# Taps' maxima in PSUM beside two tiles' results, the subtraction on VectorE, the first taps ahead of the weights' loads, and a new order

## The chip, the core and the metric

The kernel runs on one core of a Trainium2 chip. A core has five engines with instruction queues of their own that run side by side: PE (TensorE, matrix products into PSUM), DVE (VectorE), ACT (ScalarE), POOL (GpSimd) and SP (SyncE, which here issues most DMAs). Each engine takes its instructions strictly in the order in which the program lists them, and waits on semaphores for the others. PSUM has banks of 512 fp32 numbers in each of 128 partitions.

The metric is the device time of one execution in microseconds (us). Before the change it is 1347.68 us, the median of three runs (1347.58 to 1349.73).

## The reference

Two stages over 8 x 4160 = 33280 tokens of width 192: a local attention with given weights, and a feed-forward product with a gated softmax and a norm.

```python
w = exp(weight_gen - max(weight_gen))                  # over the 7 taps, for 8 heads
w = w / (sum(w) + 1e-09)
x = einsum('bshk,bskhg->bshg', w, windows(x, 7))       # each token: 7 taps over itself and its 6 predecessors

h = x @ w_in                                           # 192 -> 1024
e = exp(h - max(h))
solu = h * e / (sum(e) + 1e-09)
ln = (solu - mean(solu)) / sqrt(var(solu) + 1e-06) * g_ln
out = ln @ w_out                                       # 1024 -> 192
```

## The kernel before

A partition holds 260 consecutive tokens, and a *tile* t is the t-th token of all 128 partitions, so there are 260 tiles. Inputs come in *chunks*, of 4, 8 and 8 tiles at first and then of 16 tiles each. For each chunk `softmax_taps` (L102) makes the attention weights in seven steps, t0 to t6, in place in the tile `wt`: t0 the maximum over 7 taps (DVE, L112, into the tile `wm`), t1 the subtraction (POOL, L114), t2 the exponential (ACT, L118), t3 the sum (DVE, L120), t4 a small constant added (ACT, L122, into `wy`), t5 the reciprocal (DVE, L124), t6 the multiplication (POOL, L126).

The attention itself runs on POOL in groups of 4 tiles (2 at the start): a multiplication of seven windows of x with the taps into `pr` (L174), an addition (L180) and another into `half` (L182). DVE adds the last two parts (L433).

For each tile there follow:

- PE transposes two tiles' x at once (L450); ACT rounds a high part (L458) and DVE takes the rest (L479);
- the first product (L491, L494), 12 matmuls in three high-low pairings, into one of three buffers `h` of two PSUM banks;
- the negated maximum (DVE, L505), the exponential with its sum (ACT, L509), the product h times e (DVE, L515), the sum of squares (ACT, L521);
- a split into two fp16 halves, high (ACT, L528) and low (DVE, L532), in the tile `hl`, which a DMA transposes into `hlT` (L540);
- the second product (L580), 24 matmuls into `po`, a PSUM bank, and the scaled output (ACT, L591, into `ot`), which a DMA stores for four tiles at a time (L594).

Row norms for the chunk (`norm_x`, L136) and per-tile scales (`scales`, L544, for groups of `stat_group` tiles) are small instructions between these. The weights arrive as float64 and are turned into fp32 by DVE and ACT in pieces during the first 60 us (`float_of_double`, L232, and the steps behind it).

`po` has one buffer. The sums and norms that are needed for the weights use the same bank early on. The order of nearly all instructions is made by `issue_order` (L660): a list scheduler over estimated costs, in which a table `URGENCY` shifts the priority of each kind of step. Its result is one list of steps. Each engine's queue is that list restricted to the engine, and where two steps of different engines touch the same PSUM tile, the later one in the list waits for the earlier one. Outside that list, ahead of it, stand the first loads and, behind the weights' loads, the taps of chunk 0 (L227).

Of the kernel before, what the change touches and what calls it, by code (L numbers as in the profile page):

```python
# [9 lines left out]
F32 = mybir.dt.float32  # L10
# [16 lines left out]
def tile_kernel(ctx: ExitStack, tc: tile.TileContext, x, weight_gen, w_in, w_out, g_ln, out):  # L27
# [26 lines left out]
    ps_o = ctx.enter_context(tc.tile_pool(name="ps_o", bufs=1, space=PSUM))  # L54

    nc.scalar.preload_act_table_set("natural_log_exp_and_others")

# [44 lines left out]
    def softmax_taps(c, step):  # L102
        n = (starts[c + 1] - starts[c]) * H
        w3 = ws[c][:, : n * K].rearrange("p (n k) -> p n k", k=K)
        if step == 0:
            m = small.tile([P, TC * H], F32, name="wm", bufs=2)[:, :n]
            y = small.tile([P, TC * H], F32, name="wy", bufs=2)[:, :n]
            taps[c] = m, y
        m, y = taps[c]
        wide = [P, n, K]  # L110
        if step == 0:
            nc.vector.tensor_reduce(m, w3, axis=AX.X, op=ALU.max)  # L112
        elif step == 1:
            nc.gpsimd.tensor_tensor(  # L114
                out=w3, in0=w3, in1=m.unsqueeze(2).broadcast_to(wide), op=ALU.subtract
            )
        elif step == 2:
            nc.scalar.activation(w3, w3, AF.Exp)  # L118
        elif step == 3:
            nc.vector.tensor_reduce(m, w3, axis=AX.X, op=ALU.add)  # L120
        elif step == 4:
            nc.scalar.activation(y, m, AF.Copy, bias=1e-9)  # L122
        elif step == 5:
            nc.vector.reciprocal(y, y)  # L124
        elif step == 6:
            nc.gpsimd.tensor_tensor(  # L126
                out=w3, in0=w3, in1=y.unsqueeze(2).broadcast_to(wide), op=ALU.mult
            )
# [60 lines left out]
    w_out = w_out.bitcast(I32)  # L189
    load_x(0)  # L190
    raw_a = att.tile([P, 2 * FF], I32, name="raw_a", bufs=1)

# [32 lines left out]
    nc.vector.tensor_scalar_mul(minus, ident, -1.0)  # L225

    for step in range(TAP_STEPS):  # L227
        softmax_taps(0, step)

# [52 lines left out]
    def norm_of_first(step):  # L282
# [5 lines left out]
        elif step == 3:  # L288
            nc.scalar.activation(sq[:, 4:7], sq[:, 4:7], AF.Square)
        elif step == 4:  # L290
            first["total"] = ps_o.tile([P, 512], F32, name="po")
            nc.tensor.matmul(first["total"][:, :3], ones, sq[:, 4:7], start=True, stop=True)
        elif step == 5:
            nc.vector.tensor_reduce(
                first["total"][:, 8:9], first["total"][:, :3], axis=AX.X, op=ALU.add
            )
        elif step == 6:
            nc.scalar.activation(column, first["total"][:, 8:9], AF.Ln, scale=1.05 * FF)
            nc.scalar.activation(column, column, AF.Exp, scale=0.5)
# [27 lines left out]
    def scale_and_sum(f, step):  # L327
# [10 lines left out]
        elif step == 1:  # L338
            if f == 0:
                second["sums"] = ps_o.tile([P, 512], F32, name="po")  # L340
            for j in range(j0, j1):
# [10 lines left out]
    def prepare_second(step, half=None):  # L352
# [8 lines left out]
        elif step == 5:  # L361
            second["total"] = second["sums"][:, 256:]
            nc.tensor.matmul(second["total"][:, :NP], ones, sq[:, :NP], start=True, stop=True)
# [42 lines left out]
    def stat_group(t):  # L406

        n = 2 if t < 2 * TG else TG
        return n if t % n == n - 1 else 0


    def group(t):

        if t < TG:
            return 2 if t % 2 == 0 else 0
        return TG if t % TG == 0 else 0
# [156 lines left out]
    def second_product(t):  # L573
        hlT = hlT_of.pop(t)

        free = t >= RUN - TG and t % 2 == 1
        po = ps_h.tile([P, FF], F32, name="h") if free else ps_o.tile([P, 512], F32, name="po")
        terms = [(half, j, w) for j in range(NJ) for half, w in ((0, 0), (0, 1), (1, 0))]
# [66 lines left out]
URGENCY = dict(  # L645
    a00=3.1, a01=2.3, a02=-28.9, a03=-6.5, a04=-3.6, a10=80, a11=-25.4, a12=-13, a13=-10, a14=10.4,
    attA=85.1, attB=2.4, b0=120.9, b1=-144.6, b2=138.3, b3=-1.5, b4=54.3, c00=-28.1, c01=85.1,
    c02=6.8, c10=-25.3, c11=31.3, c12=-72.7, c20=99.4, c21=-5.6, c22=10.2, c30=-149.7, c31=-14.5,
    c32=-100.3, dup=52.6, exp=-129.5, f0=8.2, f1=-120.4, f2=-71.5, f3=-118.4, f4=-66.1, f5=-45.6,
    fin=18.4, hi=-11, lo=33, lw=18.7, lx0=10.2, lx1=-115.4, lx2=-109.1, lx3=-20.7, max=-30,  # L650
    mm1=25.5, mm2=0.4, n0=-7.5, n1=11.8, n2=-1.8, n3=-113.6, n4=-8.6, n5=-69, n6=-123.6, od=-6.9,
    out=-81.2, p30=22.9, p31=0.5, p4=9.7, p5=12.6, p6=11.6, p70=-10.2, p71=-8.7, p80=20.3, p81=5.9,
    q00=7.1, q01=-5.1, q02=118.9, q10=-15.7, q11=20.7, q12=16.8, q20=100.6, q21=-95.2, q22=20.4,
    q30=143.8, q31=81.5, q32=98.3, solu=-7.6, sq=5, t0=5.1, t1=-3.7, t2=77.9, t3=44.1, t4=-26.5,
    t5=110.1, t6=267.2, tr=-13, v00=170.9, v01=5.1, v02=44, v03=0.2, v1=54.2, v2=58.8, v3=-12.2,
    v4=1, v5=21.2, xT=-66.9, xhi=-46.7, xld=30,
)


def issue_order(run, starts, group, stat_group, loads):  # L660
# [7 lines left out]
    SAME, CROSS = (25, 127, 143, 0, 102), 130  # L668
    free = [3000, 5900, 5000, 12000, 9050]
    steps, number = [], {}  # L670
# [10 lines left out]
    for n, part in enumerate(parts):  # L681
        w_in, size = n < 3, 512 if n < 3 else 384
        at = (9000, 10500, 12000)[n] if w_in else 15000
        before = () if w_in else (f"{parts[n - 3]}4", "n" + {"a0": "0", "a1": "1", "b": "2"}[parts[n - 3]]) if n < 6 else ("q00",)
# [9 lines left out]
        else:  # L694
            f = n - 3
            once(f"q{f}0", ACT, 700, part + "2")
            once(f"q{f}1", PE, 660, f"q{f}0", *([f"q{f - 1}1"] if f else ["n6"]))
# [35 lines left out]

    add("v00", 0, ACT, 1800, ready=9000)
    add_norms(0, 0)
    for c in range(1, len(starts) - 1):
# [8 lines left out]
        for part in range(4 if whole else 1):  # L745
# [5 lines left out]
            else:  # L751
                add(f"v0{part}", t, ACT, size, ready=15000)
        add_norms(c, t)
        n = (starts[c + 1] - t) * 8
        on = (DVE, POOL, ACT, DVE, ACT, DVE, POOL)
        wide = 60 + 7.3 * n
        costs = (wide, 13.5 * n, 100 + 6 * n, wide, 100 + n, 60 + 6.3 * n, 13.5 * n)
        for k in range(7):
# [4 lines left out]
            else:  # L763
                add("t0", t, on[k], costs[k], ready=12000)

# [3 lines left out]
    for i, t in enumerate(groups):  # L769
# [4 lines left out]
        if c > 1:  # L774
            after.append((f"lx{loads - 1}", starts[c]))
        add("attA", t, POOL, 14990 if full else 7500, *after, ready=15000 if c == 1 else 9000)
        add("attB", t, POOL, 3510 if full else 1800, ("attA", t), ("fin", groups[i - 2] if i > 1 else -1))
# [21 lines left out]
    for t in range(run):  # L799
# [13 lines left out]
        add("tr", t, SP, 1792, ("lo", t), ("mm2", t - 6))  # L813
        after = [("p80", 0), ("p81", 0)] if t == 0 else []
        if t >= run - 4:
            after += [("mm1", run - 1), ("out", t - 2)]
        else:
            after.append(("out", t - 1))
        add("mm2", t, PE, 2170, ("tr", t), *after)
        add("out", t, ACT, 304, ("mm2", t), ("f5", stats_of[t]), ("od", t // 4 * 4 - 5))  # L820
        if n := stat_group(t):
# [103 lines left out]
```

## Time and profile before

| | |
|---|---|
| median of three runs | 1347.68 us |
| the profiled execution | 1347.67 us |
| its span, first to last instruction | 1345.8 us |
| mean granted TensorE clock | 0.994 |
| HBM read and written | 46.15 MB and 25.56 MB |

A row of the profile's costliest groups names the line, the engine, the operation, what it writes and reads, how often it ran, the busy us of all, the mean ns of one, and the idle time ahead of it with what ended it. Busy shares of stretches of the span (stage rows) tell where the kernel is limited by what. All durations come from the one profiled execution.

### The profile page before, as it was taken

What the parts mean: (1) busy time and instruction counts of PE and PEld (TensorE: products, weight loads), DVE (VectorE), ACT (ScalarE), POOL (GpSimd) and SP (SyncE); (2) the same over time, 40 slices, a digit from 0 to 9 for tenths busy, and PEclk for the clock granted to TensorE, in tenths of its full rate; (3) what the DMA queues carried; (4) which work ended last, traced back from release to release, by engine and by line L of the source; (5) the groups of instructions that cost most, each with busy time, mean ns of one, the idle gap of its engine ahead of it and who ended that gap; (6) DMA issues with size and microseconds to landing.
All of it is one profiled execution on the core that took longest, in us unless ns stands there. A gap on an engine that the chain in (4) does not pass through costs nothing.

```text
span 1345.8 us, 25810 instructions
## 1 busy us (share of the span) xinstructions
PE 1246.8 (93%) x9900; PEld 970.8 (72%) x9900; DVE 1210.2 (90%) x1588; ACT 1162.8 (86%) x2318; POOL 1247.7 (93%) x241
## 2 busy tenths in 40 slices
PE   0588899999999999999999999999999999999997
PEld 0365677777777777777777777777777777777776
DVE  5988899999999999999999999999999999889994
ACT  3778889889898988989898998989898898988886
POOL 5989899999999999999999999999999999999930
PEclk9899999999999999999999999999999999999999
DMA  5277668797886889688797968878787877976776
GB/s 180 74 159 169 139 134 201 123 207 137 155 179 134 196 137 208 125 179 163 129 202 140 191 140 180 162 128 203 140 193 137 183 150 138 183 134 123 133 134 130
DMA packets 565307, 210.31 MB, mean 156 GB/s; under 512 B 544456, under 2 KB 545864, under 8 KB 565184
## 3 DMA queue, kind: packets, MB, share of 16 engines
q1 hardware_dynamic: 563208, 206.55, 75.7%
q10 hardware_dynamic: 1976, 2.12, 0.6%
q8 instruction: 78, 1.28, 0.4%
q14 instruction: 45, 0.37, 0.1%
HBM read 46.15 MB, written 25.56 MB: 53 GB/s over the span
## 4 chain that ended last, share of the span: by engine, by line
ACT 43%; DVE 35%; issue 11%; PE 7%; DMA 2%; POOL 1%; SPq 0%; ACTq 0%; POOLq 0%
ACT hl L528 12%; ACT e L521 12%; DVE h L515 11%; DVE hl L532 11%; ACT e L509 9%; DVE stats L505 5%; DVE a L433 4%; ACT junk L145 3%; PE po L580 3%; PE h L494 2%; ACT x_hi L458 2%; ACT ot L591 2%; DMA hlT<-hl 2%; PE h L491 1%; DVE x_lo L479 1%
## 5 line engine op out<-in xcount | busy, mean ns | idle before, releaser
L174 POOL TENSOR_TENSOR pr<-xt,wt 128x5376 f32<-128x5376 f32 (+1 forms) x66 | 631.6, 9569 | 2.7
L580 PE MATMUL po<-w_hl,hlT 128*128 128x192 f16 x6192 | 555.1, 246 | 17.3 <-ACT ot L591 12.6
L580 PEld LDWEIGHTS <-hlT 128*128 128x128 f16 x6240 | 505.9, 98 | 83.2 <-issue 75.5
L515 DVE SCALAR_TENSOR_TENSOR h<-h,row,e 128x1024 f32<-128x1024 f32 x260 | 333.8, 1285 | 19.1 <-ACT e L509 16.9
L528 ACT ACTIVATE hl<-h 128x1024 f16<-128x1024 f32 x260 | 266.0, 1029 | 98.4 <-DVE h L515 55.4
L532 DVE SCALAR_TENSOR_TENSOR hl<-h,hl 128x1024 f16<-128x1024 f32 x260 | 316.5, 1218 | 36.8 <-ACT e L521 34.4
L180 POOL TENSOR_TENSOR pr<-pr 128x2304 f32<-128x2304 f32 (+1 forms) x66 | 333.0, 5045 | 5.2
L505 DVE TENSOR_REDUCE stats<-h 128x1 f32<-128x1024 f32 x260 | 316.3, 1217 | 3.9 <-PE h L494 3.3
L509 ACT ACTIVATE e<-h,stats 128x1024 f32<-128x1024 f32 x260 | 293.3, 1128 | 16.1 <-DVE stats L505 15.5
L521 ACT ACTIVATE e<-h,stats 128x1024 f32<-128x1024 f32 x260 | 293.0, 1127 | 1.1 <-DVE hl L532 1.0
L494 PE MATMUL h<-wa_hi,x_hi 128*128 128x512 f32 x520 | 234.0, 450 | 0.0
L182 POOL TENSOR_TENSOR half<-pr 128x1536 f32<-128x1536 f32 (+1 forms) x66 | 225.8, 3421 | 5.2
L494 PE MATMUL h<-wa_lo,x_hi 128*128 128x512 f32 x520 | 206.4, 397 | 0.0
L494 PE MATMUL h<-wa_hi,x_lo 128*128 128x512 f32 x520 | 205.9, 396 | 0.0
L494 PEld LDWEIGHTS h<-wa_hi,x_hi 128*128 128x128 f32 x520 | 98.1, 189 | 107.1 <-issue 95.5
L491 PE MATMUL h<-wb_hi,x_hi 64*128 64x512 f32 x520 | 131.0, 499 | 17.1 <-DVE hl L532 11.2
L433 DVE TENSOR_REDUCE a<-half 128x768 f32<-128x1536 f32 (+1 forms) x66 | 117.2, 1776 | 0.0
L591 ACT ACTIVATE ot<-po,stats 128x192 f32<-128x192 f32 x258 | 112.4, 436 | 3.6 <-PE po L580 3.6
L494 PEld LDWEIGHTS h<-wa_hi,x_lo 128*128 128x128 f32 x520 | 98.4, 189 | 23.2
L494 PEld LDWEIGHTS h<-wa_lo,x_hi 128*128 128x128 f32 x520 | 99.0, 190 | 12.0
L491 PE MATMUL h<-wb_hi,x_lo 64*128 64x512 f32 x520 | 104.2, 395 | 0.0
L450 PE MATMUL pa<-ident,a 128*128 128x128 f32 x520 | 81.2, 278 | 23.9 <-DVE x_lo L479 13.2
(89 smaller groups left out, 1072.0 us busy)
## 6 DMA issues: line engine op xcount, KB each, us to landing
out_dram<-ot SPq DMA_DIRECT2D x65, 384.0 KB, 3.3
xt<-in_x_dram SPq DMA_DIRECT2D x30, 576.0 KB, 4.8
xt<-in_x_dram SPq DMA_DIRECT2D x30, 480.0 KB, 4.4
wt<-in_weight_gen_dram SPq DMA_DIRECT2D x15, 448.0 KB, 4.8
hlT<-hl SPq DMA_TRANSPOSE x260, 4.7
xt<-in_x_dram SPq DMA_DIRECT2D x3, 384.0 KB, 4.6
raw_a<-in_moe_w_in_dram ACTq DMA_DIRECT2D x2, 512.0 KB, 7.4
raw<-in_moe_w_out_dram ACTq DMA_DIRECT2D x1, 768.0 KB, 12.2
```

The lines of the kernel that those rows point to most:

```text
L174: nc.gpsimd.tensor_tensor(out=window(pr, 0, [(TG * D, K), (HG, n * H), (1, HG)]), in0=window(xt, t * D, [(D, K), (HG, n * H), (1, HG)]), i ...
L180: nc.gpsimd.tensor_tensor(out=pr[:, :3], in0=pr[:, :3], in1=pr[:, 3:6], op=ALU.add)
L182: nc.gpsimd.tensor_tensor(out=half, in0=window(pr, 0, [(2 * TG * D, 2), (D, n), (1, D)]), in1=window(pr, TG * D, [(5 * TG * D, 2), (D, n), ...
L491: nc.tensor.matmul(h[:, fs], lhs[rows, 1, :], rhs[rows], start=n == 0, stop=False)
L494: nc.tensor.matmul(h[:, fs], lhs[:, 0, :], rhs[:, fs], start=False, stop=n == 2)
L505: nc.vector.tensor_reduce(stat(t, NMAX), h_of[t], axis=AX.X, op=ALU.max, negate=True)
L509: nc.scalar.activation(e, h_of[t], AF.Exp, bias=stat(t, NMAX), accum_out=stat(t, Z))
L515: nc.vector.scalar_tensor_tensor(out=h, in0=h, scalar=row(t, SCALE), in1=e, op0=ALU.mult, op1=ALU.mult, accum_out=stat(t, M))
L521: nc.scalar.activation(e_of.pop(t), h_of[t], AF.Square, bias=stat(t, M), scale=-float(FF), accum_out=stat(t, Q),)
L528: nc.scalar.activation(hl[:, 0, :], h_of[t], AF.Copy, scale=2.0**14)
L532: nc.vector.scalar_tensor_tensor(out=hl[:, 1, :], in0=h_of[t], scalar=2.0**14, in1=hl[:, 0, :], op0=ALU.mult, op1=ALU.subtract,)
L580: nc.tensor.matmul(po[:, :D], hlT[:, half * NJ + j, :], w2_hl[:, j, w, :], start=n == 0, stop=n == len(terms) - 1,)
```

## The change

One PSUM tile `results` of 512 columns, allocated once, takes the place of the buffer `po`. Columns 0 to 191 hold the second product's result of even tiles, columns 192 to 383 that of odd tiles, and columns 384 to 511 are `maxima`, in which the taps' maxima and then their sums stand. The weights' sums and norms use the same tile. The subtraction t1 moves from POOL to DVE. The seven steps of chunk 0's taps are issued right behind the loads of x, ahead of the weights' loads. The last four tiles' attention and scales come in groups of two. `URGENCY`, the cost estimates and the start times of `issue_order` are others, and in it a second product waits for the output of two tiles before, not of the tile before.

```diff
+    results = ps_o.tile([P, 512], F32, name="po")
+    maxima = results[:, 2 * D :]
...
         if step == 0:
-            m = small.tile([P, TC * H], F32, name="wm", bufs=2)[:, :n]
+            m = maxima[:, :n]
...
         elif step == 1:
-            nc.gpsimd.tensor_tensor(
+            nc.vector.tensor_tensor(
                 out=w3, in0=w3, in1=m.unsqueeze(2).broadcast_to(wide), op=ALU.subtract
             )
...
     load_x(0)
+    for step in range(TAP_STEPS):
+        softmax_taps(0, step)
     raw_a = att.tile([P, 2 * FF], I32, name="raw_a", bufs=1)
...
-    for step in range(TAP_STEPS):
-        softmax_taps(0, step)
-
...
-            first["total"] = ps_o.tile([P, 512], F32, name="po")
+            first["total"] = results[:, D:]
...
-                second["sums"] = ps_o.tile([P, 512], F32, name="po")
+                second["sums"] = results
...
-            second["total"] = second["sums"][:, 256:]
+            second["total"] = second["sums"][:, D:]
...
     def stat_group(t):
 
-        n = 2 if t < 2 * TG else TG
+        n = 2 if t < 2 * TG or t >= RUN - TG else TG
...
     def group(t):
 
-        if t < TG:
+        if t < TG or t >= RUN - TG:
             return 2 if t % 2 == 0 else 0
...
-        po = ps_h.tile([P, FF], F32, name="h") if free else ps_o.tile([P, 512], F32, name="po")
+        po = ps_h.tile([P, FF], F32, name="h") if free else results[:, t % 2 * D :]
...
 URGENCY = dict(
-    a00=3.1, a01=2.3, a02=-28.9, a03=-6.5, a04=-3.6, a10=80, a11=-25.4, a12=-13, a13=-10, a14=10.4,
+    a00=143.5, a01=29.1, a02=142.6, a03=-8.2, a04=36, a10=-15.8, a11=-124.6, a12=-13.3, a13=-148.1,
...
-    free = [3000, 5900, 5000, 12000, 9050]
+    free = [3000, 5600, 7700, 12000, 6200]
...
-        on = (DVE, POOL, ACT, DVE, ACT, DVE, POOL)
+        on = (DVE, DVE, ACT, DVE, ACT, DVE, POOL)
...
-        costs = (wide, 13.5 * n, 100 + 6 * n, wide, 100 + n, 60 + 6.3 * n, 13.5 * n)
+        costs = (wide, 60 + 7.5 * n, 100 + 6 * n, wide, 100 + n, 60 + 6.3 * n, 13.5 * n)
...
-        after = [("p80", 0), ("p81", 0)] if t == 0 else []
+        after = [("p80", 0), ("p81", 0)] if t < 2 else []
...
-            after.append(("out", t - 1))
+            after.append(("out", t - 2))
         add("mm2", t, PE, 2170, ("tr", t), *after)
-        add("out", t, ACT, 304, ("mm2", t), ("f5", stats_of[t]), ("od", t // 4 * 4 - 5))
+        add("out", t, ACT, 304, ("mm2", t), ("out", t - 1), ("f5", stats_of[t]), ("od", t // 4 * 4 - 5))
```

The new lines shift line numbers by 2 to 5: the multiplication t6 is L126 before and L129 after, the output L591 before and L593 after.

What this does to the queues is shown at three places. First POOL's queue behind its setup, which is the start of the attention. Before:

```order
L114 TENSOR_TENSOR wt<-wt,wm 128x224
L126 TENSOR_TENSOR wt<-wt,wy 128x224
L174 TENSOR_TENSOR pr<-xt,wt 128x7x384
L180 TENSOR_TENSOR pr<-pr 128x3x384
L182 TENSOR_TENSOR half<-pr 128x2x384
L114 TENSOR_TENSOR wt<-wt,wm 128x448
L174 TENSOR_TENSOR pr<-xt,wt 128x7x384
L180 TENSOR_TENSOR pr<-pr 128x3x384
L182 TENSOR_TENSOR half<-pr 128x2x384
L126 TENSOR_TENSOR wt<-wt,wy 128x448
L174 TENSOR_TENSOR pr<-xt,wt 128x5376
```

And in the changed kernel:

```order
L129 TENSOR_TENSOR wt<-wt,wy 128x224
L177 TENSOR_TENSOR pr<-xt,wt 128x7x384
L183 TENSOR_TENSOR pr<-pr 128x3x384
L185 TENSOR_TENSOR half<-pr 128x2x384
L177 TENSOR_TENSOR pr<-xt,wt 128x7x384
L183 TENSOR_TENSOR pr<-pr 128x3x384
L185 TENSOR_TENSOR half<-pr 128x2x384
L129 TENSOR_TENSOR wt<-wt,wy 128x448
L177 TENSOR_TENSOR pr<-xt,wt 128x5376
```

The two subtractions are gone from the queue; nothing else of it has moved. The multiplication by `wy` ahead of the first full group still stands where it stood.

Second, ACT's queue at the very start, where it issues DMAs beside its own work (`raw_a`, `raw` and `g` are the weights; `xt` is x). Before:

```order
L79 DMA xt<-in_x_dram 15x1152 x4
L195 DMA raw_a<-in_moe_w_in_dram 128x1024 x2
L202 DMA raw_101<-in_moe_w_out_dram 128x4x384
L206 DMA g<-in_moe_g_ln_dram 128x8x1
L118 ACTIVATE wt<-wt 128x224
L145 ACTIVATE junk,squares_x<-xt 128x1920
L122 ACTIVATE wy<-wm 128x32
```

And in the changed kernel:

```order
L82 DMA xt<-in_x_dram 15x1152 x4
L121 ACTIVATE wt<-wt 128x224
L200 DMA raw_a<-in_moe_w_in_dram 128x1024
L125 ACTIVATE wy<-po 128x32
L200 DMA raw_a<-in_moe_w_in_dram 128x1024
L207 DMA raw_110<-in_moe_w_out_dram 128x4x384
L211 DMA g<-in_moe_g_ln_dram 128x8x1
L148 ACTIVATE junk,squares_x<-xt 128x1920
```

The exponential and the copy of chunk 0's taps have moved from behind the weights' four DMA issues to ahead of them and between them.

Third, DVE's queue in the middle of the program, around tile 106, with the engines that each instruction waits for. Here is the new subtraction (L117, the chunk's t1) among the work on tiles in the changed kernel:

```order
L435 TENSOR_REDUCE a<-half 128x4x192 [waits Pool_49]
L554 TENSOR_REDUCE stats<-stats 128x4 [waits Activation_49]
L154 TENSOR_REDUCE row<-squares_x 128x1
L117 TENSOR_TENSOR wt<-wt,po 128x896 [waits Activation_49]
L507 TENSOR_REDUCE stats<-h 128x1 [waits PE_49]
L554 TENSOR_REDUCE stats<-stats 128x4 [waits DVE_49,Activation_49]
L534 SCALAR_TENSOR_TENSOR hl<-h,hl 128x1024 [waits DMAHW1_49,Activation_49]
L507 TENSOR_REDUCE stats<-h 128x1 [waits PE_49]
```

And the same chunk's maximum (L112), the last tap step of DVE ahead of the subtraction, in the kernel before:

```order
L505 TENSOR_REDUCE stats<-h 128x1 [waits PE_49]
L112 TENSOR_REDUCE wm<-wt 128x128 [waits DMAHW2_49]
L532 SCALAR_TENSOR_TENSOR hl<-h,hl 128x1024 [waits DMAHW0_49,Activation_49]
L515 SCALAR_TENSOR_TENSOR h,stats<-h,row,e 128x1024 [waits Activation_49]
L505 TENSOR_REDUCE stats<-h 128x1 [waits PE_49]
L479 TENSOR_TENSOR x_lo<-pa,x_hi 128x512 [waits Activation_49]
```

DVE has one wide instruction more per chunk. It reads `po`, the shared PSUM tile, and so waits for ACT's last output (L593) out of that tile, which the maximum before did not, as it waited for the taps' load alone.

More of the change, by code (lines that the diff above doesn't have):

```diff
@@ L645 @@
 URGENCY = dict(
-    a00=3.1, a01=2.3, a02=-28.9, a03=-6.5, a04=-3.6, a10=80, a11=-25.4, a12=-13, a13=-10, a14=10.4,
[L647 to L656, printed above, removed]
+    a00=143.5, a01=29.1, a02=142.6, a03=-8.2, a04=36, a10=-15.8, a11=-124.6, a12=-13.3, a13=-148.1,
+    a14=14.1, attA=13.6, attB=-137.4, b0=7, b1=14, b2=83.6, b3=-11.4, b4=121.6, c00=-60.9,
+    c01=-77.4, c02=-122, c10=-12.7, c11=-99.9, c12=41.6, c20=24, c21=10.1, c22=-8.8, c30=-149.2,
+    c31=-118.3, c32=19.2, dup=-8.3, exp=-147.7, f0=43.7, f1=-13.3, f2=-168.4, f3=16.9, f4=-71.9,
+    f5=-19.2, fin=101.3, hi=-5.7, lo=16.7, lw=-2.4, lx0=-55.1, lx1=8.6, lx2=-11.3, lx3=-8.4,
+    max=0.8, mm1=14.7, mm2=23.2, n0=-88.8, n1=-12.3, n2=23.1, n3=-102.1, n4=25.9, n5=82.4, n6=8.5,
+    od=34.2, out=-87.5, p30=10.9, p31=1.5, p4=-70.3, p5=105.1, p6=5.9, p70=52.9, p71=-7.8,
+    p80=78.8, p81=-0.5, q00=13.6, q01=8.1, q02=66.8, q10=-6.7, q11=87.9, q12=-135.4, q20=-113.1,
+    q21=8.7, q22=31.5, q30=-97.8, q31=-9.4, q32=123, solu=-21.2, sq=0, t0=106.9, t1=104.9,
+    t2=-145.8, t3=-20.8, t4=-55.9, t5=23.5, t6=6.9, tr=-84.7, v00=9.9, v01=14.1, v02=126.7,
+    v03=44.6, v1=112.6, v2=16.1, v3=-10.1, v4=315.6, v5=16.8, xT=8.3, xhi=-12, xld=-90.7,
 )
@@ L682, in issue_order @@
         w_in, size = n < 3, 512 if n < 3 else 384
-        at = (9000, 10500, 12000)[n] if w_in else 15000
+        at = (12000, 12000, 12500)[n] if w_in else 20000
         before = () if w_in else (f"{parts[n - 3]}4", "n" + {"a0": "0", "a1": "1", "b": "2"}[parts[n - 3]]) if n < 6 else ("q00",)
@@ L695, in issue_order @@
             f = n - 3
-            once(f"q{f}0", ACT, 700, part + "2")
+            once(f"q{f}0", ACT, 700, part + "2", "a02", "a12")
             once(f"q{f}1", PE, 660, f"q{f}0", *([f"q{f - 1}1"] if f else ["n6"]))
@@ L732, in add_norms @@
         add("v5", t, ACT, 240, ("v4", t))
-    add("v00", 0, ACT, 1800, ready=9000)
+    add("v00", 0, ACT, 1800, ready=10000)
     add_norms(0, 0)
@@ L751, in issue_order @@
             else:
-                add(f"v0{part}", t, ACT, size, ready=15000)
+                add(f"v0{part}", t, ACT, size, ready=21500)
         add_norms(c, t)
         n = (starts[c + 1] - t) * 8
-        on = (DVE, POOL, ACT, DVE, ACT, DVE, POOL)
+        on = (DVE, DVE, ACT, DVE, ACT, DVE, POOL)
         wide = 60 + 7.3 * n
-        costs = (wide, 13.5 * n, 100 + 6 * n, wide, 100 + n, 60 + 6.3 * n, 13.5 * n)
+        costs = (wide, 60 + 7.5 * n, 100 + 6 * n, wide, 100 + n, 60 + 6.3 * n, 13.5 * n)
         for k in range(7):
@@ L763, in issue_order @@
             else:
-                add("t0", t, on[k], costs[k], ready=12000)
+                add("t0", t, on[k], costs[k], ready=15500)
     groups = [t for t in range(run) if group(t)]
@@ L775, in issue_order @@
             after.append((f"lx{loads - 1}", starts[c]))
-        add("attA", t, POOL, 14990 if full else 7500, *after, ready=15000 if c == 1 else 9000)
+        add("attA", t, POOL, 14990 if full else 7500, *after, ready=21500 if c == 1 else 10000)
         add("attB", t, POOL, 3510 if full else 1800, ("attA", t), ("fin", groups[i - 2] if i > 1 else -1))
```

## Prediction

> **What bounds the kernel now.** I start with the busy shares on the page and then cut the span into stages, because an average over 1345.8 us mixes them.
>
> ```profile
> PE 1246.8 (93%) x9900; PEld 970.8 (72%) x9900; DVE 1210.2 (90%) x1588; ACT 1162.8 (86%) x2318; POOL 1247.7 (93%) x241
> ...
> 50.00:100.00 50.00, 36.11 (x235) 26.62 (x234) 41.94 (x62) 39.08 (x83) 46.24 (x11) 0.86 0.55 115
> 100.00:200.00 100.00, 88.97 (x686) 68.03 (x684) 89.06 (x115) 86.46 (x174) 92.17 (x19) 0.98 0.72 147
> 200.00:1200.00 1000.00, 974.80 (x7809) 759.34 (x7807) 925.88 (x1193) 897.45 (x1784) 985.75 (x181) 1.00 0.81 163
> 1200.00:1250.00 50.00, 50.00 (x400) 39.49 (x399) 45.12 (x58) 43.18 (x84) 49.37 (x9) 1.00 0.68 133
> ```
>
> The stage rows give busy us and (instructions) of PE, PEld, DVE, ACT and POOL, then the granted clock. PE and POOL tie on the page. In the middle POOL has 985.75 of 1000 us, PE 974.80. A tile costs PE 38 matmuls (12 first product, 24 second, 2 transposes: 9900 / 260), so 7809 of them are 205.5 tiles: 4.866 us a tile, **77.86 us per chunk of 16**. Which of the two sets that?
>
> ```profile
> L174 POOL TENSOR_TENSOR pr<-xt,wt 128x5376 f32<-128x5376 f32 x64 | 621.7, 9713 | 2.7
> L180 POOL TENSOR_TENSOR pr<-pr 128x2304 f32<-128x2304 f32 x64 | 327.7, 5121 | 5.0
> L182 POOL TENSOR_TENSOR half<-pr 128x1536 f32<-128x1536 f32 x64 | 222.2, 3471 | 5.0
> L114 POOL TENSOR_TENSOR wt<-wt,wm 128x896 f32<-128x896 f32 x15 | 26.6, 1772 | 9.7 <-DVE row L151 6.3 <-DVE wm L112 3.4
> L126 POOL TENSOR_TENSOR wt<-wt,wy 128x896 f32<-128x896 f32 x15 | 26.5, 1766 | 4.7 <-DVE stats L552 3.9 <-ACT ot L591 0.8
> ...
> PE pa L450 <- DVE x_lo L479: 8.2, 17, 0.5
> PE h L491 <- ACT e L521: 5.9, 12, 0.5
> PE h L491 <- DVE hl L532: 5.5, 12, 0.5
> PE po L580 <- ACT ot L591: 4.1, 11, 0.4
> ```
>
> A chunk asks four groups (9.713 + 5.121 + 3.471 = 18.305) and two tap steps (1.772 + 1.766) of POOL: 76.76 us. The other 1.1 are 14 gaps between instructions and the short L126 waits, so POOL is full: POOL sets the pace. PE's waits (the last four rows are its waits from 200 to 1200) are 25 us in 1000, of half a microsecond each, on four different partners; that is slack being shown somewhere. But PE is close: 0.9748 x 77.86 = 75.9 us of work per chunk, and from 1200 to 1250, where no taps are left and POOL has run ahead, PE is busy 50.00 of 50 and does 400 / 38 = 10.5 tiles, 4.75 us each, 76.0 a chunk. That is PE's floor.
>
> The Trainium skill ("Perfetto Trace Analysis", Identifying the Most-Contended Engine) calls matmul busy time a bad measure of PE's headroom and wants the weight loads' busy share. By that, 759 of 1000 would leave PE 24% of room and the middle would fall to POOL's new period without a remainder. The row 1200 to 1250 speaks against so much: there the loads are busy 79% and no tile goes through faster than 4.75 us, so 76% is near full.
>
> **The change, part by part.**
>
> *The subtraction leaves POOL.* Per chunk POOL loses one L114 (1.772) and its gap (1.1 / 14 = 0.08): 77.86 - 1.85 = **76.0 us**. This lies on the path, as POOL had no idle. What is late next is PE, with 75.9 to 76.0: both are then full.
>
> *It arrives on DVE.*
>
> ```profile
> L479 DVE TENSOR_TENSOR x_lo<-pa,x_hi 128x512 fp32r<-128x512 f32 x130 | 88.6, 681 | 4.9 <-ACT x_hi L458 4.9
> L112 DVE TENSOR_REDUCE wm<-wt 128x128 f32<-128x896 f32 x15 | 16.2, 1077 | 0.0
> L120 DVE TENSOR_REDUCE wm<-wt 128x128 f32<-128x896 f32 x15 | 16.1, 1074 | 0.0
> L122 ACT ACTIVATE wy<-wm 128x128 f32<-128x128 f32 x15 | 5.6, 371 | 0.0
> ...
> DVE stats L552 <- ACT e L521: 31.9, 39, 1.1
> DVE hl L532 <- ACT e L521: 24.5, 40, 2.1
> DVE h L515 <- ACT e L509: 12.2, 24, 0.8
> ```
>
> No row subtracts 896 elements with one operand in PSUM. L479 does 512 so in 0.681 us; in proportion 896 would take 1.19, and the reductions over the same 896 take 1.08. I take 1.1 (0.7 to 1.8, the ends being L479's 512 elements and POOL's own 1.772), as the reduction walks the same elements; at 1.8 DVE would have 73.9 of 76.0. DVE's work per chunk goes from 0.92588 x 77.86 = 72.1 to 73.2 of 76.0. That is 96%, and it is hidden only if DVE gives up half of its waits on ACT (68.6 in 1000, 5.3 per chunk). The maxima's and sums' new place costs nothing by itself.
>
> *Two results in one bank, and the order.* The order shows that every access to the one `results` tile is chained: a second product waits for the outputs or tap steps written ahead of it, and they for it. What is gained is that two second products may stand back to back and two outputs behind them; PE's 4.1 us on L591 in the row above is all that this can return in the middle, 0.3 per chunk. What may be lost is a rival below.
>
> Which period, then? Below 76.0 neither engine lets it; above, PE can keep its waits, 25.2 x 0.0779 = 2.0, and the period is 77.9. I take **76.3**, near the lower end, because the row 1200 to 1250 shows PE without a wait once POOL is not what it waits for. That is -1.55 per chunk, over 1000 / 77.86 = 12.8 chunks **-20 us**. The first 200 and the last 146 us are counted apart.
>
> *The head.*
>
> ```profile
> 8.86 0.39 ACT L118 ACTIVATE wt<-wt 128x224 f32<-128x224 f32 x1 [6.84 <-issue]
> 9.15 1.79 ACT L145 ACTIVATE junk<-xt 128x1920 f32<-128x1920 f32 x1
> 12.38 0.69 DVE L241 TENSOR_SCALAR h<-raw_a 128x512 int32<-128x512 int32 x1 [9.09 <-DMA raw_a<-in_moe_w_in_dram]
> 17.08 0.58 POOL L126 TENSOR_TENSOR wt<-wt,wy 128x224 f32<-128x224 f32 x1 [13.26 <-DVE wy L124]
> 17.73 4.95 POOL L174 TENSOR_TENSOR pr<-xt,wt 128x2688 f32<-128x2688 f32 x1
> 37.51 0.54 DVE L124 RECIPROCAL wy<-wy 128x64 f32<-128x64 f32 x1
> 39.17 9.71 POOL L174 TENSOR_TENSOR pr<-xt,wt 128x5376 f32<-128x5376 f32 x1
> ...
> POOL wt L114 <- DVE row L151: 6.3, 1, 6.3
> POOL wt L114 <- DVE wm L112: 4.3, 2, 3.4
> ```
>
> Today the first exponential (8.86) waits behind the weights' DMA issues on ACT, so the sum and the reciprocal come only between the weights' conversions on DVE and POOL multiplies from 17.73. With the taps ahead, ACT's exponential follows its last load of x, and the first attention is free when x has landed, about 9.2 (L145 reads it at 9.15). These 8 us are not all kept: the next taps' reciprocal stood 38 rows behind the first conversion and was reached at 37.51, 0.66 us a row; it now stands 29 behind, at about 31.5. So POOL waits there, multiplies, and starts the first full group near 33.5 and not 39.17: -5. Two more POOL waits, 6.3 and 3.4, were for the removed L114; if nothing replaces them the head gains 14.7. Against it: the second load of the first matrix stands behind one more ACT instruction, and two half-size subtractions fall among the conversions (at most 0.68 each, L479's price): +1.5 if POOL's gain were not used. PE is idle 13.9 + 11.0 us from 50 to 200, so it can use some. I take **-8**, halfway between the sure 5 and 14.7 less the 1.5 and a bit.
>
> *The tail.*
>
> ```profile
> 1329.37 2.14 PE L580 MATMUL po<-w_hl,hlT 128*128 128x192 f16 x24 [1.50 <-ACT ot L591]
> 1332.94 2.14 PE L580 MATMUL po<-w_hl,hlT 128*128 128x192 f16 x24 [1.43 <-ACT ot L591]
> 1339.94 2.15 PE L580 MATMUL h<-w_hl,hlT 128*128 128x192 f16 x24 [0.90 <-DMA hlT<-hl]
> ```
>
> The last four tiles' attention and scales come in pairs. POOL pays the gaps of another group, some tenths, which PE, full in the row 1200 to 1250, hides. Two waits of 1.50 and 1.43 could go, but the last product waits for its transposed tile, not for PE. **-1** (0 to -2.9).
>
> Sum against the profiled execution: 1345.8 - 20 - 8 - 1 = 1316.8 us of span; outside the span lie 1347.67 - 1345.8 = 1.87, so **1318.7 us**. The profiled 1347.67 is the median of the runs (1347.68), so no further correction.
>
> **The rivals.**
>
> *Everything falls into place.* Middle at 76.0 (-23.9), head -14.7, tail -2.9: 1306 us. For it: PE at 50.00 of 50 is possible. Against it: that was without taps and norms on DVE and ACT.
>
> *PE takes the bound over, waits and all.* The middle stays at 77.9 and only head and tail gain: 1338.7 us. For it: the waits on L479 (8.2) and on the product's buffers (11.4) have nothing to do with the subtraction. Against it: in a loop that POOL drives some engine must show waits.
>
> *DVE is the new bound.* With its 5.3 us of waits kept, 73.2 + 5.3 = 78.5 per chunk, +8 in the middle, -9 outside: 1347 us, no change. For it: DVE's waits are for ACT, which has 69.9 us of work of its own and serves in order. Against it: half of the waits suffices.
>
> *The bank turns into a queue: slower.* The maxima, subtraction and sum on DVE and the copy on ACT each need the bank while no second product writes it. If each holds a product up for its whole length, PE loses 1.08 + 1.1 + 1.07 + 0.37 = 3.6 per chunk: 75.9 + 3.6 = 79.5, +21 in the middle, 1360 us. It decides as soon as PE loses over 2.0 per chunk more than the work itself. For it: the order has such a wait in two of three second products. Against it: a second product holds the bank for 2.15 of PE's 4.75 us a tile, which leaves 2.6, longer than any of the four steps; and in the program's order only 19 of 260 outputs and 8 of 72 tap steps stand right behind the start of another tile's second product, the rest behind the start of other PE work, when the bank is free. The Trainium skill ("PSUM — Partial Sum Buffer", PSUM bank collisions raise a hardware error) wants any two engines kept apart by bank, not by address, and so speaks against this layout; no run here shows a collision, and the order shows the program keeps that rule by waits.
>
> **How the numbers follow.** Forecast 1318.7: 0.50 (its own range 1311 to 1327). All in place, 1306: 0.17. PE bound with its waits, 1339: 0.18. DVE bound, 1347: 0.06. Bank, 1360: 0.09. Faster by over 0.2% (about what a measurement can tell from no change, 2.7 us) is the first three, 0.85; the same 0.06; slower 0.09. The range 1304 to 1340 leaves out the last two and a little of the second.
>
> **What would show it.** POOL's groups without L114 and 76.0 to 76.6 us between groups 16 tiles apart; PE at over 99% in the middle; DVE at 96%. POOL's first attention at 9 to 10 us and its first full group near 33.5. Wrong would be: PE's waits on the bank's users above 2 us per chunk, DVE idle on ACT as before, or POOL idle in front of L129 (the multiplication, now the only tap step on it) again and again.

## The result and the profile after

| | before | after |
|---|---|---|
| median of four runs | 1347.63 us (1346.77 to 1349.73) | 1378.78 us (1376.96 to 1380.64) |
| ratio | 1 | 1.0229, 95% interval 1.0211 to 1.0247 |
| span of the profiled execution | 1345.8 us | 1377.1 us |
| mean granted TensorE clock | 0.994 | 0.992 |

The change makes the kernel slower by 31 us; 1318.7 was forecast, with a range up to 1340. First the busy shares and the shares of the chain that ended last (followed back from the last instruction, at each step to what released it), from the page of the changed kernel, with the chain of the kernel before behind them; then the cost of the new subtraction, from the groups by shape of the changed kernel:

```profile
PE 1255.4 (91%) x9900; PEld 979.6 (71%) x9900; DVE 1225.8 (89%) x1610; ACT 1166.7 (85%) x2323; POOL 1220.4 (89%) x226
...
PE 47%; ACT 22%; DVE 20%; issue 7%; POOL 3%; DMA 2%; SPq 0%; ACTq 0%; DVEq 0%; POOLq 0%
```

```profile
ACT 43%; DVE 35%; issue 11%; PE 7%; DMA 2%; POOL 1%; SPq 0%; ACTq 0%; POOLq 0%
```

```profile
L593 ACT ACTIVATE ot<-po,stats 128x192 f32<-128x192 f32 x258 | 108.3, 424 | 79.5 <-PE po L582 76.3 <-DVE po L123 2.6
L129 POOL TENSOR_TENSOR wt<-wt,wy 128x896 f32<-128x896 f32 x15 | 26.4, 1761 | 53.5 <-ACT stats L569 15.5 <-ACT ot L593 10.5 <-DVE wy L127 9.1
...
L117 DVE TENSOR_TENSOR wt<-wt,po 128x896 f32<-128x896 f32 x15 | 16.2, 1080 | 1.1 <-ACT ot L593 0.9
```

The subtraction takes 1.08 us on DVE, as forecast. But no engine is full any more: POOL, busy 985.75 of the 1000 us in the middle before, now waits 53.5 us in front of its multiplication L129. The chain has little of POOL in either kernel, 1% before and 3% after: before it ran through ACT and DVE, after the change it runs through PE for nearly half of the time. In front of the outputs L593 ACT waits 79.5 us, nearly all of it for a second product (L582). The same stages as in the prediction, from the windows of the changed kernel (window, busy us and instructions of PE, PEld, DVE, ACT, POOL, then the clock, the DMA share and GB/s):

```profile
100.00:200.00 100.00, 93.55 (x734) 73.34 (x734) 93.80 (x122) 86.70 (x176) 98.90 (x20) 0.98 0.75 158
200.00:1200.00 1000.00, 948.12 (x7502) 738.58 (x7503) 911.26 (x1174) 877.50 (x1741) 935.70 (x163) 1.00 0.77 158
```

7502 matmuls are 197.4 tiles: 5.065 us each, 81.05 us per chunk where it was 77.86. The waits of the changed kernel from 200 to 1200 (total us, times, longest), ACT's, PE's and POOL's:

```profile
ACT ot L593 <- PE po L582: 58.1, 60, 2.4
ACT hl L530 <- DVE h L517: 31.9, 42, 1.6
ACT e L511 <- DVE stats L507: 8.4, 17, 1.8
...
PE po L582 <- ACT ot L593: 9.2, 20, 0.9
...
PE po L582 <- ACT wy L125: 4.0, 7, 1.6
PE po L582 <- DVE po L123: 2.9, 4, 1.2
...
PE po L582 <- DVE wt L117: 2.0, 3, 1.2
PE po L582 <- DVE po L115: 1.0, 1, 1.0
...
POOL wt L129 <- ACT stats L569: 15.5, 1, 15.5
POOL wt L129 <- ACT ot L593: 10.5, 2, 5.3
```

ACT's waits before, in the same stretch:

```profile
ACT hl L528 <- DVE h L515: 40.5, 61, 1.0
ACT hl L528 <- DVE stats L552: 35.3, 38, 1.1
ACT e L509 <- DVE stats L505: 14.0, 12, 1.2
```

ACT's wait for a second product does not occur in this stretch before and is its longest after. One such place, from the timeline of the changed kernel (start, us, then the instruction, and in brackets how long the engine had been idle and for whom):

```profile
543.24 2.14 PE L582 MATMUL po<-w_hl,hlT 128*128 128x192 f16 x24 [0.45 <-DVE po L123]
...
545.41 0.28 ACT L125 ACTIVATE wy<-po 128x128 f32<-128x128 f32 x1 [1.03 <-PE po L582]
...
545.74 2.14 PE L582 MATMUL po<-w_hl,hlT 128*128 128x192 f16 x24 [0.36 <-ACT wy L125]
...
546.70 1.10 ACT L511 ACTIVATE e<-h,stats 128x1024 f32<-128x1024 f32 x1
...
547.92 1.29 DVE L517 SCALAR_TENSOR_TENSOR h<-h,row,e 128x1024 f32<-128x1024 f32 x1 [1.08 <-ACT e L511]
547.92 0.42 ACT L593 ACTIVATE ot<-po,stats 128x192 f32<-128x192 f32 x1
...
548.39 2.14 PE L582 MATMUL po<-w_hl,hlT 128*128 128x192 f16 x24 [0.51 <-ACT ot L593]
...
550.57 0.42 ACT L593 ACTIVATE ot<-po,stats 128x192 f32<-128x192 f32 x1 [1.32 <-PE po L582]
```

The three products are those of tiles 89, 90 and 91, the two outputs those of 89 and 90. Tile 89's result is ready at 545.38, but its output comes at 547.92, behind the product of tile 90. Tile 90's result is ready at 547.88, and its output stands behind the product of tile 91: ACT stops for 1.32 us with everything behind it in its queue. The taps' copy L125 stops ACT for 1.03, the exponential L511 comes as much later, and DVE stops for 1.08. The wait is handed on from engine to engine.

Over the whole run 86 of 255 outputs start after the next tile's product has ended; before it is none.

Where the 31 us lie is read from the start of DVE's maxima of single tiles (L505 before, L507 after) and the end of the last store's issue:

| us | before | after | difference | forecast |
|---|---|---|---|---|
| to tile 24 (most of the first 200 us) | 185.7 | 177.1 | -8.6 | -8 |
| tile 24 to tile 232 | 1012.7 | 1049.2 | +36.5 | -20 |
| tile 232 to the end | 144.5 | 147.8 | +3.3 | -1 |

The head's gain does not last: tile 40 starts at 264.0 before and 264.8 after. From then on POOL is far ahead and of no use: from the end of a group's last step on POOL to its first tile's maximum it took 15 to 18 us before in tiles 40 to 216, and takes 30 to 44 us after.

### The profile page after: what moved, and what is told of

The parts are those of the page before. It is cut to its first block, busy times and chain, and to the rows that moved or that the text cites. A ratio compares the mean times of both kernels' runs of the same rounds, so it can differ in the third digit from the quotient of the medians.

```text
span 1377.1 us, 25916 instructions
## 1 busy us (share of the span) xinstructions
PE 1255.4 (91%) x9900; PEld 979.6 (71%) x9900; DVE 1225.8 (89%) x1610; ACT 1166.7 (85%) x2323; POOL 1220.4 (89%) x226
## 4 chain that ended last, share of the span: by engine, by line
PE 47%; ACT 22%; DVE 20%; issue 7%; POOL 3%; DMA 2%; SPq 0%; ACTq 0%; DVEq 0%; POOLq 0%
PE po L582 24%; PE h L496 13%; PE h L493 8%; ACT e L523 7%; ACT hl L530 6%; DVE hl L534 5%; DVE h L517 5%; ACT e L511 3%; DVE stats L507 3%; PE pa L452 2%; ACT ot L593 2%; DVE a L435 2%; POOL pr L177 1%; DMA xt<-in_x_dram 1%; DVE x_lo L481 1%
## 5 line engine op out<-in xcount | busy, mean ns | idle before, releaser
L582 PE MATMUL po<-w_hl,hlT 128*128 128x192 f16 x6192 | 549.0, 246 | 28.0 <-ACT ot L593 12.3
L582 PEld LDWEIGHTS <-hlT 128*128 128x128 f16 x6240 | 513.0, 98 | 74.0 <-issue 71.3
L183 POOL TENSOR_TENSOR pr<-pr 128x2304 f32<-128x2304 f32 (+1 forms) x67 | 333.2, 4973 | 5.3
L507 DVE TENSOR_REDUCE stats<-h 128x1 f32<-128x1024 f32 x260 | 315.5, 1216 | 11.3 <-PE h L496 11.2
L511 ACT ACTIVATE e<-h,stats 128x1024 f32<-128x1024 f32 x260 | 291.4, 1121 | 22.5 <-DVE stats L507 19.8
L593 ACT ACTIVATE ot<-po,stats 128x192 f32<-128x192 f32 x258 | 108.3, 424 | 79.5 <-PE po L582 76.3
L452 PE MATMUL pa<-ident,a 128*128 128x128 f32 x520 | 85.0, 281 | 47.3 <-DVE a L435 30.2
L452 PEld LDWEIGHTS pa<-ident,a 128*128 128x128 f32 x520 | 61.1, 143 | 65.9 <-DVE a L435 26.1
```

What stands on the lines that cost most here:

```text
L183: nc.gpsimd.tensor_tensor(out=pr[:, :3], in0=pr[:, :3], in1=pr[:, 3:6], op=ALU.add)
L507: nc.vector.tensor_reduce(stat(t, NMAX), h_of[t], axis=AX.X, op=ALU.max, negate=True)
L511: nc.scalar.activation(e, h_of[t], AF.Exp, bias=stat(t, NMAX), accum_out=stat(t, Z))
L582: nc.tensor.matmul(po[:, :D], hlT[:, half * NJ + j, :], w2_hl[:, j, w, :], start=n == 0, stop=n == len(terms) - 1,)
```

## The experiments

Three theories, by the numbers that the expectations give them. 1, **the bank**: outputs wait for products that need not be ahead of them, since all users of `results` are chained in the list's order, and the scheduler does not know of that chain. 2, **DVE**: the added subtraction overloads it. 3, **the order**: the new list is poor, whatever the bank does. All kernels were timed in three rounds (the last in five) beside the kernel before. The parts of the time, as in the table above:

| | time, us | ratio to before, 95% | to tile 24 | 24 to 232 | from 232 |
|---|---|---|---|---|---|
| before | 1347.63 | 1 | 185.7 | 1012.7 | 144.5 |
| after | 1378.78 | 1.0211 to 1.0247 | 177.1 | 1049.2 | 147.8 |
| x1_out_sbuf | 1331.21 | 0.9843 to 0.9895 | 174.6 | 1008.3 | 143.9 |
| x7_after_sub_pool | 1377.71 | 1.0184 to 1.0222 | 177.6 | 1047.5 | 147.9 |
| x4_outputs_first | 1446.23 | 1.069 to 1.075 | 179.4 | 1108.4 | 155.4 |
| x9_bank_known | 1357.18 | 1.0053 to 1.0094 | 179.0 | 1024.4 | 148.1 |
| x2_max_sbuf | 1421.48 | 1.0506 to 1.0571 | 187.9 | 1080.9 | 147.9 |
| x3_no_bank | 1376.75 | 1.0182 to 1.0273 | 175.2 | 1053.5 | 143.9 |
| x5_before_sub_dve | 1358.91 | 1.0049 to 1.0102 | 191.4 | 1017.9 | 144.4 |
| x8_before_sub_psum | 1353.98 | 1.003 to 1.0063 | 187.0 | 1018.2 | 145.3 |
| x6_before_taps_first | 1344.64 | 0.9957 to 0.9978 | 182.0 | 1013.0 | 144.5 |
| y1_bank_tuned | 1339.16 | 0.9922 to 0.9949 | 170.6 | 1021.5 | 141.0 |

### The outputs out of the bank: x1_out_sbuf

```diff
-        nc.scalar.activation(ot[:, t % TG, :], po[:, :D], AF.Copy, scale=stat(t, OUT))
+        free = t >= RUN - TG and t % 2 == 1
+        src = po[:, :D] if free else wa_hi.bitcast(F32)[:, :D]
+        nc.scalar.activation(ot[:, t % TG, :], src, AF.Copy, scale=stat(t, OUT))
```

> The changed kernel with one edit: the scaled output (L593) reads a constant SBUF tile in place of the second product's result, so it no longer touches the shared PSUM bank; the output is not the reference's. Order and queues are those of the changed kernel. Theory 1 (bank: an output stands in the list behind the next tile's second product, and as both use one bank ACT waits for that product with its whole queue behind it): ACT's waits at L593 fall from 76 us to under 10, the time falls to 1330 to 1350. Theory 2 (DVE: the subtraction is one wide instruction too many) and theory 3 (the new order is poor whatever the bank): 1370 or more.

1331.21 us, 47.6 less than after, and less than before. The list, the queues and the subtraction on DVE are those of the change; the tap steps still share the bank with the products. The outputs scale a constant SBUF tile, so this kernel leaves the products' results out. The outputs' chain is gone, and from 200 to 1200 no wait at the output is left. Their true dependence is gone with it: 11 outputs start before their own product has ended, 8.6 us in all, so a part of the gain, about that much by these waits, may come from the missing data and not from the bank. The middle, in the windows of this kernel:

```profile
200.00:1200.00 1000.00, 979.47 (x7809) 768.54 (x7807) 942.12 (x1216) 912.22 (x1800) 976.28 (x169) 1.00 0.80 163
```

So DVE, 942 us busy here, is not too full, and the order alone is not poor. But 7809 matmuls are no more than before the change had in this stretch. Between tiles 40 and 216 a chunk takes 76.88 us where it took 77.83 before, 0.95 less of the 1.55 forecast; tiles 24 to 40 take 83.6 us where they took 78.3. More on that below.

### The subtraction back on POOL: x7_after_sub_pool

```diff
-            m = maxima[:, :n]
+            m = small.tile([P, TC * H], F32, name="wm", bufs=2)[:, :n]
...
-            nc.vector.tensor_tensor(
+            nc.gpsimd.tensor_tensor(
```

> The changed kernel with the subtraction back on POOL and the maxima in SBUF, list the same. Theory 2 (DVE: the subtraction is one wide instruction too many for it): 1355 or less. Theory 1 (bank): the outputs' waits remain, 1362 to 1385.

1377.71 us: as after. The list is the new one, DVE has its old work, and no tap step uses the bank, only products and outputs do. ACT's waits from 200 to 1200 in this kernel:

```profile
ACT ot L593 <- PE po L582: 55.6, 57, 2.4
```

That falsifies the theory of DVE, and it also clears the tap steps in the bank: products and outputs alone, chained in this list, make ACT wait as long. That the times agree so closely is in part chance, as POOL has the subtraction back and a wait for the maximum (L115) that the changed kernel does not have, 22.8 us from 200 to 1200.

### Which side waits: x4_outputs_first

The list's products are moved behind the previous tile's output where no engine's own queue changes by it, so that PE waits and not ACT.

```diff
-    for op, t in issue_order(RUN, starts, group, stat_group, LOADS):
+    for op, t in outputs_first(issue_order(RUN, starts, group, stat_group, LOADS)):
```

> The changed kernel with the same queue on every engine; only in the list that joins the queues a second product that stood ahead of the previous tile's output is put behind it, so PE waits for the output where ACT waited for the product. Theory 1: ACT's 76 us at L593 fall to under 15 and PE's waits at L582 on L593 grow instead; the time changes by more than 5 us, down if ACT's queue was the dearer one (1355 to 1370), up if PE's is. Theory 3: no change beyond 4 us.

1446.23 us, 67 more than after. From 200 to 1200 PE now waits for outputs 83.7 us (it was 9.2), and ACT still waits for products, 64.4, where under 15 was expected:

```profile
ACT ot L593 <- PE po L582: 64.4, 55, 3.9
...
PE po L582 <- ACT ot L593: 83.7, 71, 2.9
```

With the queues as they are, the chain costs either way, and more when PE waits.

### A list that knows of the bank: x9_bank_known

The change's kernel, table and costs; the scheduler alone learns that a user of the bank doesn't start before the last user on another engine has ended.

```diff
+        in_bank = name in ("t0", "t1", "t3", "t4") or name in ("mm2", "out") and (t < run - 4 or t % 2 == 0)
+        if in_bank and bank_on != e and bank_end + CROSS > time:
+            ready[i] = bank_end + CROSS
+            heapq.heappush(later[e], (ready[i], k, i))
+            continue
...
+        if in_bank:
+            bank_end, bank_on = end, e
```

> The changed kernel, same table and costs, with a rule added to the list scheduler: a step that uses the shared bank (second product, output, the taps' maximum, subtraction, sum and copy) does not start before the last user on another engine has ended. Theory 1 (bank): ACT's waits at L593 (line moved) fall from 76 us to under 15, the time falls by 20 to 35 us to 1343 to 1358, as the order now holds what the chip does. Theory 3 (the table's order is poor whatever the bank): 1370 or more.

1357.18 us, 21.6 less than after, with the same instructions on the chip. ACT's waits for products from 200 to 1200 fall from 58.1 to 9.0 us, and POOL's at the multiplication from 53.6 to 19.3, four rows of which the first is shown (over the whole run ACT's fall from 76.3 to 16.1, just above the 15 expected as a bound):

```profile
ACT ot L593 <- PE po L582: 9.0, 16, 1.3
...
POOL wt L129 <- DVE wy L127: 8.5, 3, 5.0
```

The loss of 31 us falls to 9. The layout is thus not wrong by itself. 94 of the first 255 outputs still start behind the next tile's product here, more than the 86 of the changed kernel, but seldom close behind it: worked out from `issue_order` in the two kernels, that product is the last of PE's steps ahead of the output in the list for 12 outputs here and for 83 in the changed kernel.

### Maxima in SBUF: x2_max_sbuf and x3_no_bank

x2 is the changed kernel with the maxima and sums in SBUF, x3 that with the edit of x1 too.

```diff
-            m = maxima[:, :n]
+            m = small.tile([P, TC * H], F32, name="wm", bufs=2)[:, :n]
```

> The changed kernel with the taps' maxima and sums in an SBUF tile again, the subtraction still on DVE; order the same. Theory 1: only the taps' part of the bank's waits goes (PE 10 us, ACT 6, DVE 6 in the 1000 us of the middle): 1362 to 1372. Theories 2 and 3: within 4 us of 1379.

> Both edits at once (outputs read a constant SBUF tile, maxima in SBUF; the output is not the reference's): no waits among users of one bank are left, with the order of the changed kernel. Theory 1: 1325 to 1342, below the kernel before. Theory 3 (poor order): 1360 or more. Theory 2: 1360 or more.

1421.48 and 1376.75 us: 43 and 46 us slower than the same kernels with the maxima in PSUM, a miss for x2, whose bank has fewer users and which got slower, and for x3, which was to be faster than the kernel before. The groups by shape, of x2 and then of x3:

```profile
L117 DVE TENSOR_TENSOR wt<-wt,wm 128x896 f32<-128x896 f32 x15 | 66.3, 4417 | 0.0
```

```profile
L117 DVE TENSOR_TENSOR wt<-wt,wm 128x896 f32<-128x896 f32 x15 | 71.6, 4774 | 0.0
```

The subtraction takes 4.4 to 4.8 us where it took 1.08. One of them in the timeline of x2:

```profile
473.51 9.70 POOL L177 TENSOR_TENSOR pr<-xt,wt 128x5376 f32<-128x5376 f32 x1
...
476.45 7.71 DVE L117 TENSOR_TENSOR wt<-wt,wm 128x896 f32<-128x896 f32 x1
...
483.29 5.81 POOL L183 TENSOR_TENSOR pr<-pr 128x2304 f32<-128x2304 f32 x1
```

DVE's subtraction starts inside POOL's multiplication, is not done when that ends at 483.21, and ends 0.87 us after POOL's next one starts. So it is in 44 of the 45 wide subtractions of x2, x3 and x5: whenever they start, they end 0.87 or 0.88 us after the start of the next POOL instruction. The one other, in x2, starts between two POOL instructions and takes 1.08 us. That fits a subtraction that gets nothing done while POOL's instruction runs. Part of the 43 and 46 us seems to come by way of PE: behind the subtraction shown PE waits 5.31 us, its next matmuls of 512 columns take 0.63 us where they had taken 0.40, and the mean granted clock of x2 and x3 is 0.974 and 0.975 (0.992 and 0.989 with the maxima in PSUM). The maxima belong in PSUM if DVE is to subtract.

### The parts alone: x5, x8 and x6

x5 is the kernel before with the subtraction on DVE and nothing else; x8 is x5 with the maxima and sums in the tile `results` too, which holds one result here. In x8 tile 255's result is written over by tile 256's before it is read; the work is the same.

```diff
-            nc.gpsimd.tensor_tensor(
+            nc.vector.tensor_tensor(
```

```diff
+    results = ps_o.tile([P, 512], F32, name="po")
+    maxima = results[:, 2 * D :]
...
-            m = small.tile([P, TC * H], F32, name="wm", bufs=2)[:, :n]
+            m = maxima[:, :n]
...
-        po = ps_h.tile([P, FF], F32, name="h") if free else ps_o.tile([P, 512], F32, name="po")
+        po = ps_h.tile([P, FF], F32, name="h") if free else results
```

> The kernel before with one edit: the subtraction on DVE, maxima in SBUF, list unchanged. If relieving POOL is worth what the prediction's sum says (period 77.9 to 76.3), 1322 to 1332. If the order, not POOL's load, holds the period: 1340 to 1350. If DVE is overloaded: over 1350.

> The kernel before with the subtraction on DVE, maxima and sums in the PSUM tile of the second product (one result at a time, as before), list unchanged. Subtraction at 1.08 us and not 2 to 4.8, as it has one operand in SBUF. If POOL's relief is worth what the prediction's sum says: period 76 to 76.6, 1322 to 1332. If the list holds the period (the steps stand on DVE where POOL's pace had put them, and POOL waits at the taps' multiplication for what it no longer does itself): period 77.8, 1345 to 1352. If four more users of the bank per chunk cost what the bank rival said (3.6 us a chunk): 1380 or more.

1358.91 and 1353.98 us, both slower than before, though POOL has a step less. Between tiles 40 and 216 a chunk takes 77.84 us in x5 and 78.30 in x8; it took 77.83. By its expectation a time over 1350 would speak for an overloaded DVE in x5; but of the 10.8 us by which its span is longer than before 10.3 are lost ahead of tile 40, and none in the period. In x8 the windows, POOL's largest wait from 200 to 1200, and the subtraction:

```profile
200.00:1200.00 1000.00, 969.36 (x7756) 754.57 (x7755) 932.86 (x1199) 891.35 (x1778) 953.85 (x166) 1.00 0.81 162
```

```profile
POOL wt L128 <- DVE stats L554: 35.1, 12, 7.6
```

```profile
L116 DVE TENSOR_TENSOR wt<-wt,po 128x896 f32<-128x896 f32 x15 | 16.3, 1088 | 7.8 <-PE po L582 7.8
```

POOL's busy time falls from 985.75 to 953.85 us, and what it saved it now waits in front of the multiplication, for DVE. In the list that multiplication stands where it stood, and so do the taps' steps on DVE and ACT among the tiles' work. The tap steps in the bank cost little by themselves: the period of x8 is 0.5 us above that of the kernel before, where the prediction's rival had 3.6.

x6 is the kernel before with chunk 0's seven tap steps moved ahead of the weights' loads.

```diff
     load_x(0)
+    for step in range(TAP_STEPS):
+        softmax_taps(0, step)
...
-    for step in range(TAP_STEPS):
-        softmax_taps(0, step)
```

> The kernel before with one edit: chunk 0's taps issued ahead of the weights' loads. If POOL's early start carries through (the prediction's head): 1338 to 1343. If the head is bound by the weights' conversion: within 2 us of 1347.6.

1344.64 us, 4.8 less than the kernel before beside it (1349.46), between the two ranges that were expected: tile 24 starts 3.7 earlier, the period stays (77.84), and here the gain is kept to the end.

### A version that beats both: y1_bank_tuned

x9 with `URGENCY` searched anew under the scheduler's new rule.

```diff
-    max=0.8, mm1=14.7, mm2=23.2, n0=-88.8, n1=-12.3, n2=23.1, n3=-102.1, n4=25.9, n5=82.4, n6=8.5,
+    max=68.2, mm1=2.0, mm2=7.3, n0=-17.2, n1=5.7, n2=30.0, n3=-26.1, n4=-21.8, n5=-52.1, n6=4.3,
...
```

> The changed kernel with the scheduler's rule for the shared bank and an URGENCY table searched anew under that rule; nothing else is changed. Theory 1 (bank): the change's parts are worth something once the order keeps the bank's users apart; ACT's waits at L593 stay under 15 us, the middle's period is 76.5 to 77.5 us a chunk, 1328 to 1342. Theory 3 (the two results and the maxima in one bank cost more than they bring whatever the order): not below 1347.

1339.16 us (1336.88 to 1340.41), 0.6% faster than before (0.5 to 0.8), the fastest of the kernels that do all the work. The gain is not where it was expected: the head gains 15.1 and the tail 3.5, the middle loses 8.7 (78.63 us per chunk, where 76.5 to 77.5 was expected). Its waits from 200 to 1200, PE's and then ACT's:

```profile
PE po L582 <- ACT ot L593: 19.8, 17, 2.4
...
ACT junk L148 <- DMA xt<-in_x_dram: 31.6, 20, 3.1
```

The products wait for outputs twice as long as in the changed kernel; ACT's largest wait is now for a load of x.

## Why the prediction was wrong

**The bank, dismissed as a rival, is what happened.** The step that failed is the count under it: "in the program's order only 19 of 260 outputs and 8 of 72 tap steps stand right behind the start of another tile's second product". With it the sum put the bank at nothing. What sets the waits is the scheduler's list, in which a product needs the output of two tiles before only. Worked out from `issue_order`, that list has 90 of 260 outputs behind the next tile's product (4 in the kernel before), 86 of them among the first 255, and on the chip just 86 of those started behind it. How 19 came about the record does not show. The rival's argument that the bank is free for 2.6 of 4.75 us is true and beside the point: an output does not look for a free moment, it waits for whatever user of the tile the list has ahead of it.

x1 gives the price: 1049.2 - 1008.3 = 40.9 us of the middle go when only the outputs leave the bank, some of them (about 8.6 by the waits) perhaps because outputs there do not wait for their own product either. x7 shows that it needs no tap step in the bank, x9 that 24.8 of it go by a list that knows of the chain. The rival had the wrong users (tap steps instead of outputs), the wrong engine and so the wrong price: +21 instead of 40.9 in the middle.

**The sign that was to tell looked at PE alone.** "PE's waits on the bank's users above 2 us per chunk": PE's five such rows, L593, L125, L123, L117 and L115, sum to 19.1 us in 1000, 1.5 per chunk, and would not have shown it. The queue formed on ACT, 58.1 us in 1000, 4.7 per chunk. The other sign held: POOL idle in front of L129 again and again, 53.6 us in 1000.

**"76.3, near the lower end" failed too, on its own.** Without the outputs in the bank the middle is 1008.3 us (x1), where 992.7 was forecast: 15.6 of the 56.5 us between forecast and result in the middle. A chunk between tiles 40 and 216 gains 0.95 us there and not 1.55, and tiles 24 to 40 lose 5.3. The reason given was that PE shows no wait from 1200 to 1250, "once POOL is not what it waits for". But POOL's relief alone, in x5 and x8, shortened nothing. The old list places the taps' chain and POOL's multiplication for the old durations, and POOL waits for the chain what it saves. Before, POOL's 985.75 of 1000 looked like the one bound; it was one of several in step, and the page of the kernel before had a sign of it, the chain that ended last, with 43% ACT, 35% DVE and 1% POOL. In their period x5 and x8 come out as the rival "PE takes the bound over, waits and all" (77.9), which had 0.18, and x1 lies between it and the forecast; that it was PE which held the period is not shown.

**The head was right where it was measured and of no use.** Forecast -8, measured -8.6 at tile 24; POOL's timeline of the changed kernel has the first full group at 33.87 (33.5 forecast) and the first attention at 7.95 (9 to 10):

```profile
7.95 4.94 POOL L177 TENSOR_TENSOR pr<-xt,wt 128x2688 f32<-128x2688 f32 x1
...
32.83 0.97 POOL L129 TENSOR_TENSOR wt<-wt,wy 128x448 f32<-128x448 f32 x1 [5.74 <-DVE wy L127]
33.87 9.70 POOL L177 TENSOR_TENSOR pr<-xt,wt 128x5376 f32<-128x5376 f32 x1
```

x6 has 3.7 of it from the taps' place alone; which parts of the change bring the other 4.9 was not separated, so that -8 was met so closely is in part luck. After, it is given back by tile 40.

**The tail**, forecast -1, is +3.3. In x1 it is -0.5 and in x3 -0.6, so the outputs' place in the bank takes this too.

**DVE** was costed rightly: 1.08 us for 1.1. As a bound it is out: x7 without the subtraction is as slow, and x1 with it is 942 us busy of 1000 at 76.88 us per chunk. That it would be 96% busy did not come, as the period grew.

**Open**: why the middle of x9 and y1, at 78.7 and 78.6 us per chunk, stays above the 77.8 before although little is left of the outputs' waits in x9. In x1, without outputs in the bank, it is 76.88 under the unimproved list. That the chain costs the remaining 1.8 by the places that it forbids is likely and was not shown. Open, too, is why tiles 24 to 40 take 83.6 us in x1 and 82.9 in x5, where they took 78.3 before.

## What to carry to other kernels

When a list scheduler sets the order, every wait that the program will have must stand in its model: two results in one PSUM tile were two buffers for the scheduler and one for the semaphores, so it must know the tile's chain before the order is searched. Waits of a shared tile are to be looked for on every engine that uses it, the reader's (ACT here) as much as the writer's. And an engine that is 98% busy under a list made for its durations need not be the only bound: remove its work alone, under the old list, before the gain is counted.

## What the runs showed of the hardware

The subtraction on DVE with both operands in SBUF ends only once POOL's running tensor instruction has ended, as if it made no progress before: 44 of 45 wide ones end 0.87 or 0.88 us after the start of the next POOL instruction, and each takes what is left of POOL's instruction and about 0.95 us more, from 1.4 us (most of x5's) to 10.1 (the longest of x2). With one operand in PSUM it takes 1.08 us beside the same POOL work. POOL pays little: L183 behind such a subtraction takes 5.81 us in the row above, where L180 took 5.12 in the mean before. The Trainium skill ("SBUF — State Buffer", Who interferes with whom) calls the port pair that VectorE and GpSimd share an exclusive lock, and says that a VectorE instruction with two SBUF inputs contends with a GpSimd instruction that reads SBUF, while one with at most one SBUF input does not, outside VectorE's 2-port modes. The rows agree: 4.4 and 4.8 us in the mean of x2 and x3 with two, 1.08 with one. x2 and x3 give the price here, 43 and 46 us, with the lower granted clock in it.
